# Last modulation row in buffers of its own, input splits at step 1, and the second new chunk packed in the new periods, in a spectral GEGLU block

## The chip, the cores and the metric

The program runs on one core of a Trainium2 chip. The metric is the device time of one execution in microseconds (us), the median of several runs of the same kernel.

## The reference, cut to what matters

```python
# x: (1, 1, 8192, 448); c: (1, 448)
mod = (silu(c) @ w_mod).reshape(1, 6, 1, 448)
sa, ca, ga, sb, cb, gb = mod[:, 0], ..., mod[:, 5]
h = layernorm(x) * (1 + ca) + sa
x = x + ga * spectral(h)          # rfft over 8192 positions, a 2-layer block MLP per frequency, irfft
h = layernorm(x) * (1 + cb) + sb
x = x + gb * ((gelu(h @ w_gate) * (h @ w_up)) @ w_down)     # 448 -> 1792 -> 448
```

`gb` is the last of the six modulation rows. It scales the output of the second half, the GEGLU network.

## The kernel before, in words

The program has four stretches. **The forward transform and the frequency MLP** go through 32 units (a half of the channels and a group of frequencies each). They are software-pipelined by `step(i)`, and `at(i, hook, fn, ...)` hangs other work on a step: loads, the scaling and splitting of the GEGLU weights into a high and a low float16 part (tiles `wk`), sums of the down weights. Steps 17 to 31 use the pool `fp` for the raw weights. `drain()` ends the pipeline.

**The turn** to the second half is straight code at the end of the listing. It finishes the inverse transform for chunk 0 in two halves of the channels: `inverse` (a matmul of the frequency data `v` with `g`), `residual`, `stats2`, `rsqrt0`, then the normalised rows `norm2` (tile `n`), `pack_hi` and `pack_lo` (the float16 high and low parts of `n` in tile `pk`), and `transposes` on TensorE into `nt`. In between stands `load_mod_row` for row 5: two DMAs into tiles `raw` of the pool `fp`, issued after the second half of the inverse, and right behind it `mod_half("gb", ...)`, eight matmuls on them. `down_hi` and `down_lo` split the down weights of one block `t` into `wd`, each in two instructions (672 and 896 elements a row).

**Eight plain chunks** (i = 0 to 7, 256 tokens each) follow. Each has 14 steps `gate_up(i, k)` of 20 matmuls (`pgu`), with a gelu on ScalarE, a product on VectorE (`x`, in `gate_up_out`), sums on GpSimd (`sums`) and `quantize` (ScalarE, then VectorE, into `ac`) for each pair of steps. After step 2 stands `down(i - 1)`: the down product of the chunk before (`pdn`), whose partial results leave through `p`, `u`, `o`. The work that prepares a coming chunk is hung on steps by the tables `hooks` (chunks 1 to 5) and `soon` (6 and 7): an entry `3: [(2, split_g), (2, split_v)]` means that after step 3 of chunk i the splits of chunk i + 2 are put into the queues. `split_g` and `split_v` cut `g` and `v` into a high part (ScalarE, `gh`, `vh`) and a low part (GpSimd, `gl`, and `v` in place); `inverse` at step 6 multiplies them in three matmuls a half (lines 1018 to 1020), the last of which takes the low part of `v`. `load_v` and `load_g` fetch the data for it.

**Twenty-four new chunks** (i = 8 to 31) use another scheme of seven periods each. `period(u)` puts its instructions into the queues in a fixed order: on TensorE 32 matmuls (`stage_a`), then later stages of the periods before, and `stage_b`, which can only follow once ScalarE has copied the bank out (`copy_b`, tile `sb`, line 1378). These chunks take more operands a row: `token_sums` makes differences of the two token halves (`tf`, VectorE and one GpSimd copy), `wpack_hi` (ScalarE) and `wpack_lo` (GpSimd) fill `pk`, and `wtransposes` issues five DMA transposes from `pk` into `nt`. The table `extra` hangs this work on the periods. Chunk 8 is the first new chunk and chunk 9 the second; before the change, both are packed at steps 12 and 13 of the plain chunks 6 and 7 (table `soon`, with `pack_rest`).

Every engine takes its instructions in the order in which the code emits them, so the tables set that order; SyncE's queue takes all DMAs. One `pk` tile serves all chunks.

Of the kernel before, what the change touches and what calls it, by code (L numbers as in the profile page):

```python
# [10 lines left out]
F32 = mybir.dt.float32  # L11
F32R = mybir.dt.float32r
F16 = mybir.dt.float16
# [6 lines left out]
D = 448  # L20
# [3 lines left out]
HC = 224  # L24
CB = 2
# [24 lines left out]
def spectral_geglu(ctx, tc, x, w1, b1, w2, b2, wg, wu, wd, cvec, wmod, cf1, cs2, cmi, cgm, out):  # L50
# [276 lines left out]
    with ExitStack() as bctx:  # L327
# [225 lines left out]
        def at(i, hook, fn, *args):  # L553
            side.setdefault((i, hook), []).append((fn, args))
# [112 lines left out]
        def load_mod_row(pool, q):  # L667
            out = []
            for hh in range(2):
                if pool is None:  # L670
                    wm = bp1.tile([128, GB, HC], F32, tag="tr", name="tr", bufs=2)[:112]
                elif callable(pool):
# [4 lines left out]
                dma(wm, wmod[:, c0 : c0 + HC].rearrange("(k p) c -> p k c", p=112))  # L677
                out.append(wm)
            return out
# [215 lines left out]
        }  # L895
        t0 = ep.tile([128, CB], F32, name="t0")

        def load_d(t, a, b):
# [46 lines left out]

        def down_lo(t):
            for r, k in zip(draws.pop(t), (slice(0, 3), slice(3, 7))):
                V.scalar_tensor_tensor(
                    wds[t][:, 1, k], r, dsc[:, t : t + 1], wds[t][:, 0, k], op0=ALU.mult, op1=ALU.subtract
                )  # L950
# [24 lines left out]
    with ExitStack() as cctx:  # L975
# [3 lines left out]
        x1s += [cp.tile([128, CB, D], F32, name=f"x1{n}") for n in (1, 2)]  # L979
        pkt = cp.tile([128, NXT * 128], F16, name="pk")  # L980
        nts, acts, pgu, outs = {}, {}, {}, []

# [60 lines left out]
        def rsqrt0(i):  # L1043

            mvt = nxt[i]["mv"]
            r, t = nxt[i]["r"][0], t0
            S.activation(r, mvt[:, :, 1], AF.Sqrt, bias=eps)
# [236 lines left out]
        def token_sums(i, part):  # L1284

            n = nxt[i]["n"]
            if part == 0:
                nxt[i]["t"] = cq.tile([128, 2 * D], F32, tag="o", name="tf") if i < NSTD + 2 else cp2.tile([128, 2 * D], F32, tag="tf", name="tf")
            t = nxt[i]["t"]
            b11, b21, x0 = n[:, 0, 0:192], n[:, 0, 192:384], n[:, 0, 384:448]  # L1290
            b12, b22, x1 = n[:, 1, 0:192], n[:, 1, 192:384], n[:, 1, 384:448]
            t1, t2, t3, t4 = (t[:, o : o + 192] for o in (0, 192, 384, 640))
            if part == 0:
                V.tensor_tensor(t1, b12, b11, ALU.subtract)
                V.tensor_tensor(t3, b22, b12, ALU.subtract)
                G.tensor_copy(t[:, 576:640], x1)
            else:
                V.tensor_tensor(t2, b22, t1, ALU.subtract)
                V.tensor_tensor(t4, b21, t2, ALU.subtract)
                V.tensor_tensor(t[:, 832:896], x0, x1, ALU.subtract)  # L1300

        def pieces(i, k):

            n, p = nxt[i]["n"], pkt
            if k == 0:
# [23 lines left out]
        def wtransposes(i, gs, w=5):  # L1329
            if i not in nts:  # L1330
                nts[i] = nt_tile()
            for g in gs:
                nc.sync.dma_start(
                    nts[i][:, w * g : w * g + w, :], pkt[:, 128 * w * g : 128 * w * (g + 1)], transpose=True
                )
# [161 lines left out]

        def pack_rest(i):
            if i == NSTD:
                wpack_hi(i, [3, 4])  # L1500
                wpack_lo(i, [3, 4])
            else:
                held.extend([(f, i, [k]) for k in (3, 4) for f in (wpack_hi, wpack_lo)])

        def pack(i):
# [124 lines left out]
        for n, k in enumerate((4, 7, 11, 13)):  # L1630
# [4 lines left out]
            5: [(1, turn)],  # L1635
            3: [(2, split_g), (2, split_v)],
            6: [(2, inverse)],
# [17 lines left out]
        soon = {  # L1655
            3: [(2, split_g), (2, split_v)],
            5: [(1, turn)],
            6: [(2, inverse)],
            7: [(2, residual)],
            8: [(2, stats2), (2, rsqrt_part, 5)],  # L1660
            9: [(2, rsqrt_part, 9)],
            10: [(2, norm2, 0)],
            11: [(2, norm2, 1)],
            12: [(2, token_sums, 0), (2, wpack_hi, [0, 1]), (2, wpack_lo, [0, 1])],
            13: [(2, token_sums, 1), (2, wpack_hi, [2]), (2, wpack_lo, [2]), (2, pack_rest)],
        }

# [67 lines left out]
        for i in range(NSTD):  # L1735
# [4 lines left out]
            for k in range(NFT):  # L1740
# [14 lines left out]
                if k == 4:  # L1755
                    store_out()
                if (i, k) == (NSTD - 1, 9):
                    load_v(NSTD + 2)
                    load_g(NSTD + 2)
                for fn, *args in first.pop(i * NFT + k, []):  # L1760
                    fn(*args)
                if k == (3, 1, 0)[min(i, 2)] and i + 2 < nch:
                    load_v(i + 2)
                    load_g(i + 2)
                for d, fn, *args in (hooks if i < NSTD - 2 else soon).get(k, []):
                    if i + d > 2 and i > 0 and i + d < nch:
                        fn(i + d, *args)
# [7 lines left out]
        sets = [sets[(n - U0) % 3] for n in range(3)]  # L1775
        pdn = [psum2.tile([128, 512], F32, name=f"pdn{n}") for n in range(2)]
        x1s.append(cp2.tile([128, CB, D], F32, name="x13"))

        for u in range(U0, NT_ + 1):
            period(u)  # L1780
# [5 lines left out]
            flush()  # L1786
            for d, fn, *args in extra[k]:
                if i + d < nch:
# [88 lines left out]
```

## Time and profile before

| | us |
|---|---|
| median of 3 runs | 1911.73 (1910.2 to 1912.13) |
| the profiled execution's own time | 1911.48 |
| its span | 1909.7 |
| TensorE busy in the span | 1858.1 |
| VectorE, GpSimd, ScalarE busy | 1433.6, 1264.3, 995.4 |
| the turn: first to last matmul of the inverse for chunk 0 to the first `pgu` | from 368.20 to 384.88 |
| the plain chunks' last `pgu` to the first matmul of the new scheme | from 770.00 to 773.83 |

Times in the trace are us from the start of the span. A row of the timeline gives the start, the time from start to end, the engine, the source line, what it writes and reads, how many instructions are merged in it, and in brackets the idle time of the engine before it with what ended that. Rows of the waits give the waiting line, what it waited for, the total, the number of waits and the longest. A row of the windows gives a stretch, its length, the busy time of the engines and, behind them, the TensorE clock that was granted (1.00 is full speed), the share of the DMA engines and GB/s.

### The profile page before, as it was taken

To read this page: it belongs to the slowest core of one execution; us is meant where nothing else is said; L and a number is where in the kernel's file an instruction comes from. 1 tells how busy PE (TensorE), PEld (TensorE's weight loads), DVE (VectorE), ACT (ScalarE), POOL (GpSimd) and SP (SyncE) were. 2 spreads that over 40 slices of the span, in tenths; PEclk is the share of its full clock that TensorE was granted. 3 is DMA by queue.
4 is the path that set the end of the run, shared out by engine and by line. 5 is a ranking of instruction groups with operands and counts; after the bars stand their busy time and mean duration, and the time that the engine had idled before them with its cause. 6 is when DMAs were issued, how large, how long until landed. Compare 5 with 4: busy or idle time off the path is not lost.

```text
span 1909.7 us, 56500 instructions
## 1 busy us (share of the span) xinstructions
PE 1858.1 (97%) x23332; PEld 1756.6 (92%) x23332; DVE 1433.6 (75%) x2888; ACT 995.4 (52%) x1843; POOL 1264.3 (66%) x1616
## 2 busy tenths in 40 slices
PE   7899999899999999899999999999999999999998
PEld 3599999778888888899999999999999999999998
DVE  8677788778766667577777777777777777777645
ACT  5687888653444444345545555555555454444443
POOL 3157655247777777577777777777777777777533
PEclk9999999999999999899999999999999999999999
DMA  9998777645434445866666665556666666666641
GB/s 353 319 291 260 203 181 196 172 135 141 104 101 102 101 90 132 230 178 175 171 180 176 177 167 166 166 166 166 167 175 179 168 176 178 169 182 178 156 140 54
DMA packets 380602, 330.49 MB, mean 173 GB/s; under 512 B 110772, under 2 KB 358712, under 8 KB 380344
## 3 DMA queue, kind: packets, MB, share of 16 engines
q1 hardware_dynamic: 380344, 326.87, 61.6%
q8 instruction: 183, 3.00, 0.6%
q14 instruction: 75, 0.61, 0.1%
HBM read 243.32 MB, written 60.10 MB: 159 GB/s over the span
## 4 chain that ended last, share of the span: by engine, by line
PE 78%; DVE 7%; POOL 5%; DMA 4%; issue 3%; ACT 2%; SPq 1%; ACTq 0%; POOLq 0%; DVEq 0%
PE set L1350 38%; PE pgu L1118 8%; PE pdn L1193 6%; PE pdn L1191 6%; PE pdn L1192 6%; PE set L1191 2%; PE set L1193 2%; PE set L1192 2%; PE ps L210 2%; DMA xt<-in_A_x 2%; DVE y L471 1%; POOL v L115 1%; DMA s<-cs 1%; POOL yl L115 1%; PE set L1460 1%
## 5 line engine op out<-in xcount | busy, mean ns | idle before, releaser
L1350 PE MATMUL set<-nt,wk 128*128 128x128 f16 x13104 | 745.4, 220 | 8.8 <-DVE x L1159 3.8
L1350 PEld LDWEIGHTS <-wk 128*128 128x128 f16 x13104 | 738.6, 98 | 13.7 <-issue 11.6
L1193 PE MATMUL pdn<-wd,ac 128*128 128x224 f16 x1218 | 316.4, 260 | 1.8 <-DVE ac L1425 1.2
L1191 PE MATMUL pdn<-wd,ac 128*128 128x224 f16 x1218 | 316.6, 260 | 0.7 <-ACT ac L1415 0.6
L1192 PE MATMUL pdn<-wd,ac 128*128 128x224 f16 x1218 | 316.4, 260 | 0.0
L1118 PE MATMUL pgu<-nt,wk 128*128 128x256 f16 (+1 forms) x2464 | 268.2, 274 | 2.7 <-DVE x L1159 2.6
L1118 PEld LDWEIGHTS <-wk 128*128 128x128 f16 (+1 forms) x2464 | 225.7, 98 | 43.7 <-issue 17.9
L1399 ACT ACTIVATE gl<-c,dg 128x384 f32<-128x384 f32 x168 | 103.6, 616 | 253.5 <-DVE c L1393 252.4
L1425 DVE SCALAR_TENSOR_TENSOR ac<-x,sa_act,ac 128x896 f16<-128x896 f32 x168 | 211.5, 1259 | 14.7 <-ACT ac L1415 14.7
L1167 POOL TENSOR_TENSOR x<-x 128x128 f32<-128x128 f32 x223 | 136.3, 611 | 118.2 <-DVE x L1159 50.7
L1234 POOL TENSOR_TENSOR o<-u,p 128x224 f32<-128x224 f32 x32 | 21.0, 658 | 260.6 <-DVE u L1233 260.6
L1403 DVE TENSOR_TENSOR x<-c,gl 128x384 f32<-128x384 f32 x168 | 175.9, 1047 | 17.1 <-ACT gl L1399 17.1
L1415 ACT ACTIVATE ac<-x,sa_act 128x896 f16<-128x896 f32 x168 | 173.7, 1034 | 3.4 <-DVE x L1170 0.4
L1170 POOL TENSOR_TENSOR x<-x 128x128 f32<-128x128 f32 x223 | 170.6, 765 | 0.1
L1191 PEld LDWEIGHTS <-ac 128*128 128x128 f16 x1568 | 153.6, 98 | 5.9 <-issue 4.8
L1193 PEld LDWEIGHTS <-ac 128*128 128x128 f16 x1568 | 153.6, 98 | 2.8 <-DVE ac L1425 1.7
L1192 PEld LDWEIGHTS <-ac 128*128 128x128 f16 x1568 | 153.6, 98 | 0.6 <-issue 0.3
L1169 POOL TENSOR_TENSOR x<-x 128x128 f32<-128x128 f32 x223 | 148.3, 665 | 0.0
L1387 DVE TENSOR_TENSOR c<-set,sb 128x512 f32<-128x512 f32 x168 | 114.9, 684 | 43.1 <-PE set L1350 43.1
L1154 ACT ACTIVATE gel<-pgu,dg 128x256 f32<-128x256 f32 x112 | 49.9, 471 | 158.3 <-PE pgu L1118 148.3
L471 DVE SCALAR_TENSOR_TENSOR y<-pm,t 64x224 f32<-64x224 f32 x256 | 99.4, 388 | 39.1 <-ACT t L463 35.1
L1168 POOL TENSOR_TENSOR x<-x 128x128 f32<-128x128 f32 x223 | 113.8, 510 | 17.5
(323 smaller groups left out, 3992.2 us busy)
## 6 DMA issues: line engine op xcount, KB each, us to landing
wk<-wk SPq DMA_DIRECT2D x76, 1024.0 KB, 9.4
wk<-wk SPq DMA_DIRECT2D x76, 768.0 KB, 5.7
tr<-td SPq DMA_DIRECT2D x64, 224.0 KB, 4.5
vd<-us SPq DMA_DIRECT2D x64, 224.0 KB, 3.2
xx<-in_A_x SPq DMA_DIRECT2D x32, 448.0 KB, 5.9
v<-vd SPq DMA_DIRECT2D x63, 224.0 KB, 5.2
out<-x SPq DMA_DIRECT2D x31, 448.0 KB, 3.6
xt<-in_A_x SPq DMA_DIRECT2D x15, 896.0 KB, 16.5
```

The source lines that it names most:

```text
L471: V.scalar_tensor_tensor(y[ri * 64 : ri * 64 + 64, gi], pv[si, ri], LAM, tv[si, ri], op0=ALU.add, op1=ALU.min)
L1118: T.matmul(pgu[i, t, q][:, pr * H : (pr + 1) * H], ws[rows, n, w, tw], nts[i][rows, tn, :], start=start, stop=stop, skip_group_check=True,)
L1167: e.tensor_tensor(s1, a21, a22, ALU.add)
L1169: e.tensor_tensor(s3, a11, a21, ALU.subtract)
L1170: e.tensor_tensor(s4, a12, s2, ALU.subtract)
L1191: T.matmul(ps, ac[:, 0, ka], w[:, 0, kb], start=n == 0, stop=False)
L1192: T.matmul(ps, ac[:, 0, ka], w[:, 1, kb], start=False, stop=False)
L1193: T.matmul(ps, ac[:, 1, ka], w[:, 0, kb], start=False, stop=n == NP - 1)
L1350: T.matmul(ps2[:, pr, reg * 128 : reg * 128 + 128], slot[:, pr, hl, wt, :], nt[:, xt, :], start=start and j == 0, stop=j == len(terms) - 1 ...
L1403: V.tensor_tensor(xs[u][:, 1::3, :], cts.pop(u)[:, 1], gls.pop(u), ALU.mult)
L1415: S.activation(ac[:, 0], xs[u][:, 0:7], AF.Copy, scale=sa_act[:, t : t + 1])
L1425: V.scalar_tensor_tensor(ac[:, 1], xs.pop(u)[:, 0:7], sa_act[:, t : t + 1], ac[:, 0], op0=ALU.mult, op1=ALU.subtract)
```

## The change

- Row 5 of the modulation weights gets two tiles of its own (`gbw`, in the pool `fp`) and its two DMAs stand in step 29.
- `rsqrt0` runs a Gelu on two elements a row right behind its Sqrt (into `g0`, which nothing reads).
- In the turn, `norm2`, `pack_hi` and `pack_lo` of chunk 0 stand ahead of the loads for what follows, and the second instruction of `down_lo(0)` stands behind `pack_lo`.
- In the plain chunks the splits stand at step 1 in place of step 3, and the loads for them at step 9 of the chunk before (chunk 3 keeps its places).
- `token_sums` and packing of chunk 8 stand at steps 0 and 1 of chunk 7; statistics and normalisation of chunks 8 and 9 stand one step later each.
- Chunk 9 is packed in periods 0 and 1 of chunk 8 (table `opening`), into a second tile `pk2`; from then on the two `pk` tiles take turns. Its five transposes stand together in period 2.

```diff
+        gbw = [fp.tile([112, 4, HC], F32, name=f"gbw{h}") for h in range(2)]
+        at(29, "load", pre, gbw, "gb", load_mod_row, 5)
...
             S.activation(r, mvt[:, :, 1], AF.Sqrt, bias=eps)
+            S.activation(g0, mvt[:, :, 1], AF.Gelu_apprx_tanh)
...
-        down_lo(0)
+        down_lo(0, range(1))
         inverse(0, halves[1])
-        pre(fp, "gb", load_mod_row, 5)
         for hh in range(2):
             mod_half("gb", gb, hh)
         residual(0, halves[1])
         stats2(0, halves[1])
         rsqrt0(0)
+        for b in range(CB):
+            norm2(0, b)
+        pack_hi(0)
+        pack_lo(0)
+        down_lo(0, range(1, 2))
         fctx.close()
...
         for t in (1, 2):
             load_d8(t)
-        for b in range(CB):
-            norm2(0, b)
-        pack_hi(0)
         S.copy(gb_r, gb[:, :D])
-        pack_lo(0)
...
         hooks = {
-            3: [(2, split_g), (2, split_v)],
+            1: [(2, split_g), (2, split_v)],
...
         soon = {
-            3: [(2, split_g), (2, split_v)],
+            0: [(1, token_sums, 0), (1, token_sums, 1), (1, wpack_hi, range(3)), (1, wpack_lo, range(3))],
+            1: [(1, wpack_hi, [3, 4]), (1, wpack_lo, [3, 4]), (2, split_g), (2, split_v)],
...
-            10: [(2, norm2, 0)],
-            11: [(2, norm2, 1)],
-            12: [(2, token_sums, 0), (2, wpack_hi, [0, 1]), (2, wpack_lo, [0, 1])],
-            13: [(2, token_sums, 1), (2, wpack_hi, [2]), (2, wpack_lo, [2]), (2, pack_rest)],
+            11: [(2, norm2, 0)],
+            12: [(2, norm2, 1)],
...
-                if k == (3, 1, 0)[min(i, 2)] and i + 2 < nch:
+                if (i, k) in ((0, 3), (1, 1)):
                     load_v(i + 2)
                     load_g(i + 2)
+                if i == 1 and k == 3:
+                    split_g(3)
+                    split_v(3)
+                if k == 9 and i > 0:
+                    load_v(i + 3)
+                    load_g(i + 3)
...
+        pkts.append(cp2.tile([128, NXT * 128], F16, name="pk2"))
...
+        opening = {
+            0: [(2, split_v), (1, token_sums, 0), (1, token_sums, 1), (1, wpack_hi, [0, 1]), ...],
+            1: [(2, split_g), (1, wpack_hi, [3]), (1, wpack_lo, [3]), (1, wpack_hi, [4]), (1, wpack_lo, [4])],
+            2: [(1, wtransposes, range(5))],
+        }
...
-            for d, fn, *args in extra[k]:
+            for d, fn, *args in opening[k] if i == NSTD and k < 3 else extra[k]:
```

How the order of the instructions moves is seen at three places. The first is ScalarE's queue in the turn, from the copy of the row `ga` to the first gelu of the plain chunks (`r` is the Sqrt of `rsqrt0`, `pk` the packing, `nt` the copy of a transpose, `wd` from `dr` the down weights of blocks 1 and 2). Before:

```order
L1692 COPY ga_r<-psm 128x224
L1047 ACTIVATE r_3372<-mv_3371,eps 128x2
L1073 CAST pk<-n_5824 128x448 x2
L1712 COPY gb_r<-psm 128x448
L1111 CAST nt<-ptr 128x512 x2
L944 ACTIVATE wd_5740<-dr,dsc 128x672
L944 ACTIVATE wd_5740<-dr,dsc 128x896
L944 ACTIVATE wd_5741<-dr,dsc 128x672
L944 ACTIVATE wd_5741<-dr,dsc 128x896
L1154 ACT_TABLE_LOAD
L1154 ACTIVATE gel<-pgu,dg 128x256 x4
```

And after:

```order
L1695 COPY ga_r<-psm 128x224
L1053 ACTIVATE r_3372<-mv_3371,eps 128x2
L1054 ACT_TABLE_LOAD
L1054 ACTIVATE g_3374<-mv_3371 128x2
L1080 CAST pk<-n_5801 128x448 x2
L1716 COPY gb_r<-psm 128x448
L1118 CAST nt<-ptr 128x512 x2
L947 ACTIVATE wd_5745<-dr,dsc 128x672
L947 ACTIVATE wd_5745<-dr,dsc 128x896
L947 ACTIVATE wd_5746<-dr,dsc 128x672
L947 ACTIVATE wd_5746<-dr,dsc 128x896
L1161 ACTIVATE gel<-pgu,dg 128x256 x4
```

The load of the activation table has moved from ahead of the first gelu to ahead of the packing.

The second is GpSimd's queue around `down(5)` in the plain chunk 6: `wr` and `wf` are sums for the new scheme's weights, `o` and the `x` of 448 elements the end of the down product, the `x` of 128 elements the sums of a pair of steps. Before:

```order
L1532 TENSOR_TENSOR wr<-wr,wf 128x384
L1533 TENSOR_TENSOR wf<-wr,wf 128x384
L1234 TENSOR_TENSOR o<-u_10013,p_10012 128x224
L1205 TENSOR_TENSOR o<-o,gb_r 128x448
L1206 TENSOR_TENSOR x_5747<-o,x_5747 128x448
L1205 TENSOR_TENSOR o<-o,gb_r 128x448
L1206 TENSOR_TENSOR x_5747<-o,x_5747 128x448
L1167 TENSOR_TENSOR x_10007<-x_10007 128x128
L1168 TENSOR_TENSOR x_10007<-x_10007 128x128
L1169 TENSOR_TENSOR x_10007<-x_10007 128x128
L1170 TENSOR_TENSOR x_10007<-x_10007 128x128
L115 TENSOR_TENSOR gl<-g,gh 128x256
```

And after:

```order
L115 TENSOR_TENSOR gl<-g,gh 128x256
L115 TENSOR_TENSOR v<-v,vh 128x896
L1535 TENSOR_TENSOR wr<-wr,wf 128x384
L1536 TENSOR_TENSOR wf<-wr,wf 128x384
L1241 TENSOR_TENSOR o<-u_10022,p_10021 128x224
L1212 TENSOR_TENSOR o<-o,gb_r 128x448
L1213 TENSOR_TENSOR x_5752<-o,x_5752 128x448
L1212 TENSOR_TENSOR o<-o,gb_r 128x448
L1213 TENSOR_TENSOR x_5752<-o,x_5752 128x448
L1174 TENSOR_TENSOR x_10016<-x_10016 128x128
```

The two low parts, `gl` and `v`, have moved from behind eleven instructions to ahead of them.

The third is ScalarE's queue where the new scheme opens (`ac` is the quantizing of the last pair of plain steps, `sb` the copies of three periods, `set` the seed copies, `vh` and `gh` the split for chunk 10). Before:

```order
L1178 ACTIVATE ac<-x_11246,sa_act 128x896
L1321 CAST pk<-n_11213 128x256
L1178 ACTIVATE ac<-x_11284,sa_act 128x896
L1321 CAST pk<-tf 128x2x192
L1321 CAST pk<-tf 128x2x256
L1378 COPY sb<-set_11343 128x512
L113 CAST vh<-v 128x896
L1382 COPY set_11343<-set_11343 128x2x128
L1378 COPY sb<-set_11344 128x512
```

And after:

```order
L1185 ACTIVATE ac<-x_11245,sa_act 128x896
L1185 ACTIVATE ac<-x_11284,sa_act 128x896
L1388 COPY sb<-set_11331 128x512
L113 CAST vh<-v 128x896
L1392 COPY set_11331<-set_11331 128x2x128
L1331 CAST pk_11336<-n_11259 128x192
L1331 CAST pk_11336<-n_11259 128x256 x2
L1388 COPY sb<-set_11332 128x512
L113 CAST gh<-g 128x256
L1392 COPY set_11332<-set_11332 128x2x128
L1331 CAST pk_11336<-tf 128x2x192
L1331 CAST pk_11336<-tf 128x2x256
```

The casts of the packing have moved from ahead of the first `sb` to behind it. GpSimd's queue has moved in the same way: its four packing instructions that stood ahead of the last pair's sums, and the others, now stand behind them.

More of the change, by code (lines that the diff above doesn't have):

```diff
@@ L896, in spectral_geglu @@
         t0 = ep.tile([128, CB], F32, name="t0")
+        g0 = ep.tile([128, CB], F32, name="g0")
         def load_d(t, a, b):
@@ L944, in down_hi, with down_lo @@
                 S.activation(wds[t][:, 0, k], r, AF.Copy, scale=dsc[:, t : t + 1])
-        def down_lo(t):
-            for r, k in zip(draws.pop(t), (slice(0, 3), slice(3, 7))):
+        def down_lo(t, ns=range(2)):
+            for r, k in list(zip(draws[t], (slice(0, 3), slice(3, 7))))[ns.start : ns.stop]:
                 V.scalar_tensor_tensor(
@@ L980, in spectral_geglu @@
         pkt = cp.tile([128, NXT * 128], F16, name="pk")
+        pkts = [pkt]
         nts, acts, pgu, outs = {}, {}, {}, []
@@ L1287, in token_sums @@
             if part == 0:
-                nxt[i]["t"] = cq.tile([128, 2 * D], F32, tag="o", name="tf") if i < NSTD + 2 else cp2.tile([128, 2 * D], F32, tag="tf", name="tf")
+                nxt[i]["t"] = cq.tile([128, 2 * D], F32, tag="o", name="tf") if i < NSTD + 1 else cp2.tile([128, 2 * D], F32, tag="tf", name="tf")
             t = nxt[i]["t"]
@@ L1300, in token_sums, with pk_of @@
                 V.tensor_tensor(t[:, 832:896], x0, x1, ALU.subtract)
+        def pk_of(i):
+            return pkts[max(0, i - NSTD) % 2]
         def pieces(i, k):
-            n, p = nxt[i]["n"], pkt
+            n, p = nxt[i]["n"], pk_of(i)
             if k == 0:
@@ L1333, in wtransposes @@
                 nc.sync.dma_start(
-                    nts[i][:, w * g : w * g + w, :], pkt[:, 128 * w * g : 128 * w * (g + 1)], transpose=True
+                    nts[i][:, w * g : w * g + w, :], pk_of(i)[:, 128 * w * g : 128 * w * (g + 1)], transpose=True
                 )
@@ L1496, in spectral_geglu @@
         }
[L1498 to L1503, printed above, removed]
         def pack(i):
@@ L1776, in spectral_geglu @@
         pdn = [psum2.tile([128, 512], F32, name=f"pdn{n}") for n in range(2)]
+        pkts.append(cp2.tile([128, NXT * 128], F16, name="pk2"))
         x1s.append(cp2.tile([128, CB, D], F32, name="x13"))
+        opening = {
+            0: [
+                (2, split_v),
+                (1, token_sums, 0),
+                (1, token_sums, 1),
+                (1, wpack_hi, [0, 1]),
+                (1, wpack_lo, [0, 1]),
+                (1, wpack_hi, [2]),
+                (1, wpack_lo, [2]),
+            ],
+            1: [(2, split_g), (1, wpack_hi, [3]), (1, wpack_lo, [3]), (1, wpack_hi, [4]), (1, wpack_lo, [4])],
+            2: [(1, wtransposes, range(5))],
+        }
         for u in range(U0, NT_ + 1):
```

14 lines of the change are left out of this document (8 added, 6 removed).

## The prediction, made before the changed kernel ran

> **What bounds the kernel now.** I read the waits of TensorE first, then the timeline around each of the three edits, engine by engine.
>
> ```profile
> PE psm L683 <- DMA raw<-in_w_mod: 6.0, 1, 6.0
> PE set L1350 <- DVE x L1159: 3.8, 1, 3.8
> PE pi L1020 <- POOL v L115: 3.6, 7, 0.6
> PE set L1350 <- ACT sb L1378: 3.6, 1, 3.6
> PE pgu L1118 <- DVE x L1159: 2.6, 1, 2.6
> ```
>
> By the table above TensorE is busy for 1858.1 us of the span of 1909.7, so only its pauses can be won, and a slow clock behind them. The rows give five such waits: one in the turn (6.0), one behind it that the turn's work feeds (2.6), seven short ones in the plain chunks (3.6 together) and two at the opening of the new scheme (3.8 and 3.6). Together they are 19.6 us; each edit stands beside one of them. The question is how much of each remains because something else is nearly as late.
>
> **The turn.** TensorE's and SyncE's rows:
>
> ```profile
> 377.85 5.49 PE L683 MATMUL psm<-raw,cs 112*128 112x224 f32 x16 [5.99 <-DMA raw<-in_w_mod]
> ...
> 384.88 7.76 PE L1118 MATMUL pgu<-nt,wk 128*128 128x256 f16 x68
> ...
> 408.55 16.66 PE L1118 MATMUL pgu<-nt,wk 128*128 128x256 f16 x140 [2.58 <-DVE x L1159]
> ```
>
> ```profile
> 372.60 1.34 SPq L677 DMA_DIRECT2D raw<-in_w_mod  x2
> ...
> 383.41 0.37 SPq L899 DMA_DIRECT2D dr<-in_B_w_down  x1
> ```
>
> The row gb was issued at 372.60 and its matmuls began at 377.85. With the load at step 29 they follow the inverse at once, and the 5.99 us are gone as a wait. They are not gone from the end: the transposes of `pk` come next on TensorE, and they wait for VectorE.
>
> ```profile
> 380.31 0.55 DVE L1082 TENSOR_TENSOR pk<-n,pk 128x384 f16<-128x384 f32 x1
> ...
> 389.99 1.15 DVE L948 SCALAR_TENSOR_TENSOR wd<-dr,dsc,wd 128x896 f16<-128x896 f32 x1 [1.87 <-ACT wd L944]
> ...
> 393.75 0.79 DVE L1159 TENSOR_TENSOR x<-pgu,gel 128x256 f32<-128x256 f32 x2 [0.36 <-ACT gel L1154]
> ```
>
> The last low part of `pk` was done at 380.31 + 0.55 = 380.86. The part of `down_lo(0)` that leaves the front of this queue has the 896 elements a row of 389.99, 1.15 us there (1.1 below), so `pk` is complete at about 379.8. Then the moved instruction runs, to 380.9, and VectorE's cast of the transposed rows into `nt` is queued behind it. Before, the first `pgu` came 1.54 us after the end of the matmuls for gb (377.85 + 5.49 = 383.34, then 384.88); that gives 379.8 + 1.5 = 381.3, and 0.7 more for the cast that waits behind the moved instruction: 382.0, 2.9 us earlier.
>
> What that is worth at the end is decided by the 2.58 us at 408.55, where TensorE waits for VectorE again. So the term goes by VectorE's chain, which begins with the down weights `dr`.
>
> ```profile
> 375.21 0.29 ACT L1047 ACTIVATE r<-mv,eps 128x2 f32<-128x2 f32 x1 [4.19 <-DVE mv L1041]
> ...
> 378.29 0.57 ACT L1073 CAST pk<-n 128x448 f16<-128x448 f32 x1 [2.79 <-DMA raw<-in_w_mod]
> ...
> 388.91 1.79 ACT L944 ACTIVATE wd<-dr,dsc 128x896 f16<-128x896 f32 x2 [1.75 <-DMA dr<-sd]
> ...
> 391.95 1.28 ACT L1154 ACT_TABLE_LOAD   x1
> ...
> 393.25 0.84 ACT L1154 ACTIVATE gel<-pgu,dg 128x256 f32<-128x256 f32 x2
> ```
>
> ScalarE waits for `dr` (1.75 at 388.91) and VectorE for ScalarE (1.87 at 389.99). The first of these loads was issued at 383.41, behind the gb row. Now it waits for the moved low part, at about 381.0: 2.4 us earlier, and the chain with it. The table load no longer lies between the last `wd` and the first gelu; VectorE was only kept idle by it for 0.36 us (393.75), since its own `wd` work ended then. That adds 0.4. At its new place the table load is covered: the Sqrt ends 1.1 us earlier, at 374.4; 1.28 and a Gelu of 0.29 (the Sqrt's row has the same size) end at 376.0, ahead of the first cast to `pk`, due at 378.29 - 1.1 = 377.2. If that cover were gone, the whole Gelu and load would cost 1.6.
>
> The Trainium skill ("ScalarE: Activation LUTs", section "What ACT_TABLE_LOAD costs") counts some 1.3 us for a load and about as much for the drain ahead of it. The trace shows the 1.28, and the gelu 0.02 behind it; a drain would show as idle time and there is none here. By the page ScalarE would be ready at about 377.4, 0.2 late, and the term would be 2.6.
>
> The 0.8 MB of early gb load falls in units 29 and on; what it could delay there I take as nothing, as the raw weights of that stretch are issued some microseconds ahead of their use, and a delay of the last would show in the turn's first matmuls. Sum of the turn: **2.8 us**. Lower bound 0.7: the slow clock after the pause.
>
> ```profile
> 377.85:382.80 4.95, 4.95 (x15) 0.55 0.76 228
> 409.00:413.00 4.00, 4.00 (x24) 0.58 1.04 222
> 774.00:785.00 11.00, 7.42 (x79) 0.54 0.88 279
> ```
>
> These windows give the length, TensorE's busy time, the granted clock, DMA share and GB/s. After a pause TensorE runs at 0.55 for 4.95 us, 2.2 us of loss. Now the pause lies between gb and the transposes, so part of this loss falls on the first `pgu`: 2.9 - 2.2 = 0.7. Upper bound 4.5: if the stall of 408.55 gets too short to slow the clock, the 0.42 x 4.0 = 1.7 us of the second row go as well.
>
> **The plain chunks.** One inverse of chunk 6, and GpSimd's rows:
>
> ```profile
> 701.70 0.45 PE L1018 MATMUL pi<-vh,gh 128*128 128x448 f32 x1
> 701.99 0.37 PE L1019 MATMUL pi<-vh,gl 128*128 128x448 f32 x1
> 702.88 0.47 PE L1020 MATMUL pi<-v,gh 128*128 128x448 f32 x1 [0.53 <-POOL v L115]
> ```
>
> ```profile
> 689.63 1.10 POOL L1533 TENSOR_TENSOR wf<-wr,wf 128x384 f32<-128x384 f32 x1 [3.69 <-DVE ws L1568]
> ...
> 700.05 0.73 POOL L115 TENSOR_TENSOR gl<-g,gh 128x256 fp32r<-128x256 f32 x1
> 700.73 2.09 POOL L115 TENSOR_TENSOR v<-v,vh 128x896 fp32r<-128x896 f32 x1
> ```
>
> The third product starts 0.89 us after the second, which started 0.29 after the first; without the wait the spacing would be 0.29, so 0.60 a chunk. The low part ended at 700.73 + 2.09 = 702.82, and the third product came 0.06 later. Six of the seven waits go, since chunk 3 keeps its places: 6 x 0.60 = **3.6 us**; by the idle time alone 6 x 3.6/7 = 3.1; if the seventh went too, 4.2. Cover: the two low parts (0.73 + 2.09 = 2.8 us) now stand ahead of `wr`, `wf` and the down product's `o` on GpSimd, where it idled 3.69 us ahead of 689.63. If that gap were filled, the sums of the next pair would be 2.8 later. The loads: a step is 20 matmuls, at 7.76/68 = 0.114 each 2.3 us, and from step 9 to step 1 are six steps, 13.7 us; the gb row above, issued at 372.60, was in use 5.25 us later. On SyncE they stand ahead of later loads and wait for the buffer that step 6 of the same chunk releases, three steps earlier.
>
> **The opening.** TensorE, VectorE, GpSimd and ScalarE:
>
> ```profile
> 773.83 2.67 PE L1350 MATMUL set<-nt,wk 128*128 128x128 f16 x32 [3.83 <-DVE x L1159]
> ...
> 780.07 11.14 PE L1350 MATMUL set<-nt,wk 128*128 128x128 f16 x154 [3.58 <-ACT sb L1378]
> ...
> 806.43 23.76 PE L1350 MATMUL set<-nt,wk 128*128 128x128 f16 x419
> ```
>
> ```profile
> 772.57 0.34 DVE L1294 TENSOR_TENSOR tf<-n 128x192 f32<-128x192 f32 x1
> 773.37 0.41 DVE L1159 TENSOR_TENSOR x<-pgu,gel 128x256 f32<-128x256 f32 x1
> ```
>
> ```profile
> 772.59 0.64 POOL L1170 TENSOR_TENSOR x<-x 128x128 f32<-128x128 f32 x1
> ...
> 774.78 1.30 POOL L1167 TENSOR_TENSOR x<-x 128x128 f32<-128x128 f32 x1
> ```
>
> ```profile
> 777.58 1.04 ACT L1178 ACTIVATE ac<-x,sa_act 128x896 f16<-128x896 f32 x1 [2.98 <-POOL x L1170]
> 778.53 1.01 ACT L1321 CAST pk<-tf 128x384 f16<-128x384 f32 x2
> 779.45 0.57 ACT L1378 COPY sb<-set 128x512 f32<-128x512 f32 x1
> ```
>
> ```profile
> 769.00:782.00 13.00, 0.00 (x0) 0.00 (x0) 0.00 (x0) 2.04 (x5) 4.72 (x7) 0.73 0.98 312
> ```
>
> The last product of the plain chunks began at 773.37, behind the differences `tf` of chunk 9, which began at 772.57. Without them it starts 0.80 earlier and ends at 773.0; the first seed matmul goes with it. The sums began at 774.78, behind packing on GpSimd. Now they can begin when the sums of the pair before end, 772.59 + 0.64 = 773.2: 1.6 earlier, and so ScalarE's `ac`, which waited 2.98 us for them. Then come two casts less ahead of `sb`, 779.45 - 778.53 = 0.9. So `sb`, and TensorE at 780.07, come 1.6 + 0.9 = **2.5 us** earlier, at about 777.6. The seed matmuls that `sb` copies end at 773.0 + 2.7 = 775.7, in time. Next late is GpSimd's sums. Lower bound 0.9, the casts alone, if sums go no faster. Upper bound 4.2, with half of what the slow clock takes at 774 to 785 (7.42 x 0.46 = 3.4) won; only half, since the first wait there shrinks from 3.83 to about 3.0 and remains.
>
> The packing comes back in the next two periods: the last window row (tile `pk`: TensorE's two, VectorE's, ScalarE's and GpSimd's busy time) has 2.04 us of ScalarE and 4.72 of GpSimd. TensorE's stretch of 154 matmuls is 11.14 us long; both fit beside it. If they did not, all 2.04 would return through `sb` and only 0.5 would remain.
>
> **The sum.** 2.8 + 3.6 + 2.5 = 8.9. The profiled execution took 1911.48 us, of which 1909.7 is the span; 1911.48 - 8.9 = **1902.6 us**. It lies 0.25 below the median of the runs shown, whose spread is 1.9, so I correct nothing.
>
> **The rivals.**
>
> *The clock no longer drops* (chance 0.25). The stalls get shorter: at 408.55 to 2.58 + 2.9 - 2.8 = 2.7 at most, and to 0.5 if the slow clock takes its 2.2 us earlier, from the first `pgu`. For it: with waits of 0.53 us the plain chunks show no such loss. Against: 2.58 was enough to give the 0.58 of 409 to 413. It would bring 1.7 there and 1.7 at the opening: 1902.6 - 3.4 = 1899.2 us. The Trainium skill ("TensorE: Matmul & The Clock Gate", section "What's actually happening") has the array idle for about a whole 3.4 us window before the clock is lowered. By that rule a stall of 2.58 us would do nothing; the measured 0.58 behind it speaks against reading it so strictly.
>
> *The moved splits cost what they win* (0.10). The 2.8 us on GpSimd delay the end of the down product or the sums, and TensorE waits 0.6 a chunk elsewhere. Against: the 3.69 us idle. All of 3.6 is lost: 1906.2 us.
>
> *The turn gains nothing* (0.10). The edit does not do what it says: the inputs of the `dr` loads come from elsewhere than the issue at 383.41, and VectorE's chain arrives as before; an earlier first `pgu` then only lengthens the stall. For it: that stall exists. 1902.6 + 2.8 = 1905.4 us.
>
> *Chunk 9's transposes come too late* (0.05; the other side).
>
> ```profile
> 792.08 7.92 SPq L1333 DMA_TRANSPOSE nt<-pk  x4
> ...
> 809.08 0.53 SPq L1269 DMA_DIRECT2D wk<-wk  x1
> ```
>
> They now stand together in period 2. If a weight load that waits for its buffer (as that at 809.08) stood ahead of them on SyncE, the third, at 7.92/4 = 1.98 each, would start at 809.1 + 4.0 + 2.0 = 815.0. The seed matmuls of chunk 9 follow 806.43 and need it 2.7 earlier, at 803.7, by the 2.7 us that 32 of them take: 11.3 us of wait and, as after the turn, 2.2 of clock, 1902.6 + 13.5 = 1916.1 us. It decides from a third transpose issued some 9 us late, 812.6. Against: the order of the code has the load that waits behind the five; they wait for GpSimd's packing alone, done by about 788.
>
> **How the numbers follow.** My forecast has 0.50, the rivals 0.25, 0.10, 0.10 and 0.05. A measurement of this kernel can tell 0.2%, 3.8 us, from no change: 1907.9 and 1915.5. The forecast by its bounds: lower ends of turn and opening together give 1902.6 + 2.1 + 1.6 = 1906.3, upper ends of all three 1911.5 - 4.5 - 4.2 - 4.2 = 1898.6. The range 1897.5 to 1907.5 holds this, the clock's rival with 1.7 more, and the two at 1905 to 1906 alone; outside are the last rival and combinations of the two lost terms. Faster by over 0.2% are all but these: 0.90; within 0.2% are the combinations, 0.05; slower 0.05.
>
> **What would show it.** In the turn: gb's matmuls without a wait, then a pause until about 379.8 and the first `pgu` near 382; `dr` issued near 381; the wait on VectorE near 405.8. In the plain chunks: one wait of L1020's kind in place of seven, and no new wait at the down product. At the opening: `sb` right behind `ac`, and TensorE resuming 2.5 us sooner than the shift so far gives. It is wrong if `dr` isn't earlier, if GpSimd's sums start as late as before, or if a new wait stands at the seeds of chunk 9.

## The result, and the profile after

The changed kernel takes 1904.06 us (median of 5 runs, 1902.93 to 1905.44) beside 1911.73 of the kernel before; the ratio is 0.9961, with a 95% interval of 0.9946 to 0.9975. Run again later it gave 0.9966 (0.9953 to 0.9978). The forecast was 1902.6, 8.9 us less than before; measured are 7.7 less. The profiled execution is the fastest of the five, 1902.93 us with a span of 1901.1. Of the runs below, one of the eleven with the turn alone took 4517.27 us, far from all others, and is left out of its ratio.

TensorE's waits after:

```profile
PE ptr L1107 <- ACT pk L1080: 4.5, 2, 3.5
PE pdn L1198 <- DVE u L1234: 3.6, 2, 2.1
PE set L1360 <- DVE x L1166: 3.3, 1, 3.3
PE pgu L1125 <- DVE x L1166: 1.8, 1, 1.8
...
PE set L1360 <- ACT sb L1388: 0.7, 1, 0.7
PE pi L1026 <- POOL v L115: 0.6, 1, 0.6
```

The wait for gb is gone (a wait for `pk` stands in its place), the seven for `v` are one, and `sb` is down from 3.6 to 0.7 (2.3 in the second trace of this kernel, see below). A new one stands second: 3.6 us in two waits of the down product for `u`.

To see where time went, I cut both traces at the same instructions. Before:

```profile
368.96 1.68 PE L683 MATMUL psm<-tr,cs 112*128 112x224 f32 x8
456.37 0.45 PE L1018 MATMUL pi<-vh,gh 128*128 128x448 f32 x1
752.63 0.36 PE L1018 MATMUL pi<-vh,gh 128*128 128x448 f32 x1
791.02 0.45 PE L1460 MATMUL set<-vh,gh 128*128 128x448 f32 x1
1864.72 0.66 POOL L1234 TENSOR_TENSOR o<-u,p 128x224 f32<-128x224 f32 x1 [13.37 <-DVE u L1233]
1903.57 0.67 POOL L1234 TENSOR_TENSOR o<-u,p 128x224 f32<-128x224 f32 x1 [6.74 <-DVE u L1233]
```

And after:

```profile
369.04 1.68 PE L685 MATMUL psm<-tr,cs 112*128 112x224 f32 x8
453.59 0.45 PE L1024 MATMUL pi<-vh,gh 128*128 128x448 f32 x1
748.31 0.36 PE L1024 MATMUL pi<-vh,gh 128*128 128x448 f32 x1
784.09 0.45 PE L1470 MATMUL set<-vh,gh 128*128 128x448 f32 x1
1858.12 0.66 POOL L1241 TENSOR_TENSOR o<-u,p 128x224 f32<-128x224 f32 x1 [13.36 <-DVE u L1240]
1895.33 0.67 POOL L1241 TENSOR_TENSOR o<-u,p 128x224 f32<-128x224 f32 x1 [5.22 <-DVE u L1240]
```

The cuts are the last matmuls for ga, the inverse of chunk 3, that of chunk 9 (second half), that of chunk 10, and the last two `o` of the program. Five stretches lie between them. Here they are for every trace of this study; a difference of starts in each case:

| | start to ga | turn | plain chunks | opening | new chunks | tail |
|---|---|---|---|---|---|---|
| before | 368.96 | 87.41 | 296.26 | 38.39 | 1073.70 | 38.85 |
| before, again | 371.33 | 88.20 | 296.34 | 37.31 | 1073.87 | 37.21 |
| changed | 369.04 | 84.55 | 294.72 | 35.78 | 1074.03 | 37.21 |
| changed, again | 370.02 | 85.35 | 293.02 | 35.13 | 1074.02 | 38.82 |
| turn alone | 369.39 | 84.40 | 296.36 | 38.32 | 1073.99 | 38.78 |
| splits alone | 368.94 | 87.41 | 291.58 | 37.43 | 1074.06 | 37.21 |
| opening alone | 370.14 | 87.31 | 296.10 | 35.73 | 1074.15 | 37.21 |
| `tf` first | 371.75 | 84.08 | 292.15 | 35.13 | 1074.00 | 38.78 |
| own gb buffers alone | 372.20 | 83.62 | 296.23 | 37.65 | 1073.80 | 38.85 |
| `down_lo` whole | 371.71 | 83.59 | 293.00 | 35.27 | 1073.78 | 37.21 |
| no Gelu ahead | 370.26 | 85.62 | 294.71 | 35.72 | 1073.98 | 37.21 |
| first combination | 370.48 | 81.63 | 297.10 | 35.15 | 1074.00 | 38.78 |
| `down_lo` and `tf` | 371.70 | 84.14 | 292.16 | 35.14 | 1073.99 | 38.85 |
| second combination | 371.51 | 82.20 | 295.83 | 33.51 | 1073.99 | 38.83 |

Between the first traces of before and after the turn gives 2.9, the plain chunks 1.5, the opening 2.6, and the tail 1.6, where the change does nothing. The start and the tail differ between two executions of one kernel by as much (368.96 and 371.33; 38.85 and 37.21): that is chance, and the other columns carry the comparison. They are not free of it either: the turn of two traces of one kernel differs by 0.8 us, the opening by up to 1.1.

### The profile page after: what moved, and what is told of

Its sections match the earlier page's. It is cut to its first block, busy times and chain, and to the rows that moved or that the text cites. A ratio compares the mean times of both kernels' runs of the same rounds, so it can differ in the third digit from the quotient of the medians.

```text
span 1901.1 us, 56363 instructions
## 1 busy us (share of the span) xinstructions
PE 1855.4 (98%) x23332; PEld 1756.8 (92%) x23332; DVE 1428.5 (75%) x2888; ACT 996.1 (52%) x1844; POOL 1266.1 (67%) x1616
## 4 chain that ended last, share of the span: by engine, by line
PE 78%; DVE 11%; DMA 4%; ACT 2%; POOL 2%; SPq 2%; issue 1%; ACTq 0%; DVEq 0%; POOLq 0%
PE set L1360 34%; PE pgu L1125 11%; PE pdn L1198 6%; PE pdn L1200 6%; PE pdn L1199 6%; PE set L1198 2%; PE set L1200 2%; PE set L1199 2%; PE ps L210 2%; DMA xt<-in_A_x 2%; DVE y L471 1%; DVE x L1413 1%; DMA raw<-in_B_w_up 1%; DVE c L1397 1%; DVE wk L826 1%
```

## The experiments

**One part at a time.** Three kernels have one part of the change each; a fourth is the changed kernel with one exchange in the table `soon`:

```diff
-            0: [..., (1, wpack_hi, range(3)), (1, wpack_lo, range(3))],
-            1: [(1, wpack_hi, [3, 4]), (1, wpack_lo, [3, 4]), (2, split_g), (2, split_v)],
+            0: [..., (1, wpack_hi, [3, 4]), (1, wpack_lo, [3, 4])],
+            1: [(1, wpack_hi, range(3)), (1, wpack_lo, range(3)), (2, split_g), (2, split_v)],
```

*The turn alone.*

> The kernel before with the turn's edits alone (own gb buffers, Gelu behind the Sqrt, packing ahead of the loads, down_lo divided). Theory: VectorE's chain from the dr loads sets the gain, so TensorE resumes at about 406.1 where it waited until 408.55, 2.4 us earlier; a further 1.7 us appear where the clock stays full behind that stall, but 1.3 of it are given back as a wait for u at the first down product. Net 2.8 us, about 1908.9. Rival: the turn's whole advance, 4.1 us, stays to the end, about 1907.6.

Measured: 1908.87 us, 0.9980 (0.9971 to 0.9989). The medians can't choose between 2.8 and 4.1 us: the ratio's interval is 2.1 to 5.5 us. The trace speaks for the theory: its turn is 3.0 us shorter than before's, and the wait at the first down product is there (1.4).

*The splits alone.*

> The kernel before with the splits at step 1 and their loads at step 9 alone. Theory: 0.78 us for each of six inverses, 4.7 us, about 1907.0, and no new wait at the down products. Rival 1 (the forecast): 0.60 each, 3.6 us, 1908.1. Rival 2: GpSimd's 2.8 us ahead of the down product's end cause the new wait of 2.1 us for u in chunk 7, so that the gain is only 1.6 us, 1910.1.

Measured: 1904.42 us, 0.9960 (0.9948 to 0.9973), more than any theory. In the stretch of the plain chunks it is 296.26 - 291.58 = 4.7 us, as the theory has it, with no wait for `u` in chunk 7. The rest of its trace's lead is 1.0 us at the opening and 1.6 in the tail, both places where the clock differs. What else the runs have in their favour stays open.

*The opening alone.*

> The kernel before with the packing edits alone (chunk 8 at steps 0 and 1 of chunk 7, chunk 9 in the new periods, second pk tile). Theory: the first output of the down product in chunk 7 has to wait for the buffer in which the differences tf of chunk 8 lie until GpSimd has packed them; that costs 3.1 us, the opening itself gains 2.5, so it is slower by 0.6 us, about 1912.3. Rival (the forecast): only the 2.5 us gain, 1909.2, and no wait for u in chunk 7.

Measured: 1908.38 us, 0.9976 (0.9967 to 0.9985). Faster, so the theory's sum was wrong.

```profile
736.98 0.39 DVE L1220 TENSOR_TENSOR o<-pdn,p 128x224 f32<-128x224 f32 x1 [5.50 <-POOL pk L1331]
```

```profile
738.94 0.26 PE L1192 MATMUL pdn<-wd,ac 128*128 128x224 f16 x1 [0.57 <-DVE u L1228]
```

VectorE does wait for `tf`'s packing ahead of the `o` of `down(6)`, 5.50 us, but TensorE waits for `u` only 0.57, about as long as before waits there for `ac` (0.62 in all). The plain chunks take 296.10 us, no more than before's 296.26: the buffer costs only where the splits have moved too. Why is seen behind `o`: two instructions `ws` take 1.29 us here, and GpSimd runs `wr` beside them.

```profile
737.29 1.29 DVE L1572 SCALAR_TENSOR_TENSOR ws<-wr,sww,ws 128x128 f16<-128x128 f32 x2
```

```profile
736.90 1.01 POOL L1536 TENSOR_TENSOR wr<-wr,wf 128x384 f32<-128x384 f32 x1
```

*`tf` first.*

> The changed kernel with chunk 8's two packing groups exchanged: the pieces from tf at step 0, those from the normalised rows at step 1. The same work on GpSimd and ScalarE, but the buffer of tf is free some 4 us earlier. Theory (the buffer): VectorE's wait of 5.5 us ahead of the first output of down(6) shrinks to about 1 us, the 2.1 us wait for u goes with the slow clock behind it, 3.1 us less than the changed kernel, about 1901. Rival (GpSimd is simply too full there): nothing changes, about 1904.

Measured: 1902.49 us, 0.9948 (0.9936 to 0.9961). The two kernels' rows for the buffer, the changed kernel first:

```profile
726.92 2.17 POOL L1337 TENSOR_TENSOR pk<-tf,pk 128x128 f16<-128x128 f32 x3
729.73 2.12 POOL L115 TENSOR_TENSOR v<-v,vh 128x896 fp32r<-128x896 f32 x1
```

```profile
729.12 0.39 DVE L1226 TENSOR_TENSOR o<-pdn,p 128x224 f32<-128x224 f32 x1 [5.49 <-POOL pk L1337]
729.43 2.84 DVE L1571 SCALAR_TENSOR_TENSOR ws<-wr,sww,ws 128x128 f16<-128x128 f32 x2
732.19 0.38 DVE L1234 TENSOR_TENSOR u<-pdn,p 128x224 f32<-128x224 f32 x1
```

```profile
732.62 0.26 PE L1198 MATMUL pdn<-wd,ac 128*128 128x224 f16 x1 [2.12 <-DVE u L1234]
```

```profile
728.00:735.00 7.00, 4.88 (x46) 0.90 0.01 3
735.00:738.00 3.00, 3.00 (x23) 0.66 0.94 197
```

With `tf` first:

```profile
723.92 2.18 POOL L1337 TENSOR_TENSOR pk<-tf,pk 128x128 f16<-128x128 f32 x3
```

```profile
729.05 0.39 DVE L1226 TENSOR_TENSOR o<-pdn,p 128x224 f32<-128x224 f32 x1
```

```profile
727.52 0.27 PE L1200 MATMUL pdn<-wd,ac 128*128 128x224 f16 x1 [1.17 <-DVE ac L1186]
```

The tile `tf` of chunk 8 and the output `o` of a down product share one buffer (`tag="o"`). In the changed kernel GpSimd ends the packing from `tf` at 729.09, VectorE's `o` follows at 729.12 after 5.49 us without work, then `ws` (2.84), and `u` comes at 732.19, for which TensorE stands still for 2.12 us; the two windows (length, TensorE's busy time, clock) show the slow clock behind. The two `ws` take 1.55 us longer (2.84) than in the kernel with the opening alone, and by as much (2.12 against 0.57) TensorE's wait is longer. The second of them takes 2.42 us in the four traces in which the moved split `v` runs on GpSimd beside it (the changed kernel twice, `down_lo` whole, no Gelu ahead), and 0.60 to 0.81 in the ten others; it ends 0.4 us after `v` (732.27 and 731.85). So the wait needs both edits; that `v` slows `ws` is read from this agreement alone, as no run moves `v` by itself. In the other order the packing ends at 726.1 and `o` has almost no wait (0.13), at the same work; `v` then runs behind both `ws`, and TensorE waits 1.17 us for `ac` in place of 2.12 for `u`. The plain chunks take 292.15 us, against 294.72 and 293.02 in the changed kernel: the order costs 0.9 to 2.6 us, the larger where the clock drops behind the wait.

**The clock.** The kernel before, unchanged:

> The kernel before once more, unchanged. In its first trace the last 39 us took 38.85 us from the last-but-one to the last o, with the clock at 0.8 behind two waits of 0.6 and 1.0 us; the changed kernel's trace has 37.21 with the same waits at full clock. Theory (the clock behind such waits is chance of the execution): the tail comes out at 37.2 or 38.8, and the clock behind the wait of 2.58 us at 408.5 full or slow, independently of the kernel. Rival (it belongs to the kernel): 38.85 and the slow clock at 409 to 413 again.

Measured: 1912.15 us (one run). The rival falls: the tail took 37.21 us and the clock behind the wait was full.

```profile
411.87 1.36 PE L1118 MATMUL pgu<-nt,wk 128*128 128x256 f16 x11 [2.58 <-DVE x L1159]
```

```profile
411.90:416.00 4.10, 4.10 (x38) 1.00 0.95 240
```

The wait for VectorE was 2.58 us again, as in the trace that had 0.58 behind it; the window (length, TensorE's busy time, clock) has 1.00. In the tail the two waits (0.6 and 1.0) are in all traces; the windows of TensorE behind them in the first trace of before, and in the changed kernel:

```profile
1892.00:1900.00 8.00, 6.88 (x53) 0.79 0.04 14
```

```profile
1885.00:1893.00 8.00, 6.82 (x68) 1.00 0.04 14
```

Eight of the fourteen traces have the long tail, six the short one. The wait for `u` of 2.1 us in chunk 7 shows the same: in the first trace of the changed kernel and without the Gelu ahead the clock behind it is 0.6 and the plain chunks take 294.7 us, in the second trace and with `down_lo` whole it is 1.00 and they take 293.0.

**The turn's parts.** The kernel before with the own gb buffers and nothing else:

```diff
+        gbw = [fp.tile([112, 4, HC], F32, name=f"gbw{h}") for h in range(2)]
+        at(29, "load", pre, gbw, "gb", load_mod_row, 5)
...
-        pre(fp, "gb", load_mod_row, 5)
```

> The kernel before with the own buffers of the gb row alone, nothing else moved. Theory: the loads dr are freed by gb's matmuls, so they start at about 376.3 in place of 383.4, ScalarE's and VectorE's wd work follows the nt casts without a wait, the stall at 408.5 goes and TensorE's earlier start by some 2.4 us stays: 4 to 5 us at 408.5, more than the whole turn's 2.4, because nothing is queued ahead of dr. Rival (the forecast's order of causes): the packing sets the first pgu and the dr loads gain nothing by it alone, at most 1 us.

And the changed kernel with `down_lo(0)` whole, at its old place:

> The changed kernel with down_lo(0) whole at its old place. Theory: the dr loads wait in the changed kernel for the moved instruction alone (381.44, issue at 381.53); whole, they start at about 376.3, the stall of 1.77 us at 406.1 goes, and TensorE gains 1.5 to 2 us there although pk is up to 0.6 us later. Rival: pk 1.1 us later delays the first pgu by as much, and the loads are no earlier: 1 us slower.

Measured: 1908.09 us, 0.9977 (0.9968 to 0.9986), and 1902.24, 0.9942 (0.9929 to 0.9954). SyncE's first `dr` in the changed kernel, with the VectorE instruction that frees it, then in the two others:

```profile
381.53 0.37 SPq L902 DMA_DIRECT2D dr<-in_B_w_down  x1
```

```profile
380.30 1.14 DVE L951 SCALAR_TENSOR_TENSOR wd<-raw,dsc,wd 128x896 f16<-128x896 f32 x1
```

```profile
379.06 0.42 SPq L901 DMA_DIRECT2D dr<-in_B_w_down  x1
```

```profile
378.56 0.42 SPq L902 DMA_DIRECT2D dr<-in_B_w_down  x1
```

Counted from the ga matmuls, `dr` starts after 12.5 us in the changed kernel, 14.4 before, 6.9 in both others. So the moved half of `down_lo(0)` holds the `dr` loads back. The turn is 83.6 us in both, 0.9 to 1.8 less than in the changed kernel, but this gain is hardly clear of chance: over all traces, those with `down_lo(0)` whole and own buffers have 81.6 to 84.1 (83.6 to 84.1 where nothing else in the turn is moved), those with all the turn's edits 84.1 to 85.4, and the ratio of the own buffers alone (0.9977) can't be told from that of the whole turn (0.9980). The stall that was to go is still there, 1.07 us in both. Neither gives the 4 to 5 us, or the 1.5 to 2, in full, since TensorE then waits at the first down product for `u` (1.72 and 1.40 us), which VectorE's normalisation of chunk 2 sets: the first combination below moves it, and has no such wait.

The changed kernel without the Gelu ahead:

> The changed kernel without the Gelu behind the Sqrt, so that the table load stands ahead of the first gelu again. Theory: ScalarE's first gelu comes 1.28 us later, VectorE's first product only 0.4 us later, since its own wd work ends then: 0.4 us at the wait near 406. Rival: the load lies on the path, 1.3 us there or, with a drain of the engine, 2.6.

```profile
391.68 1.28 ACT L1160 ACT_TABLE_LOAD   x1
392.97 0.84 ACT L1160 ACTIVATE gel<-pgu,dg 128x256 f32<-128x256 f32 x2
```

```profile
393.48 0.79 DVE L1165 TENSOR_TENSOR x<-pgu,gel 128x256 f32<-128x256 f32 x2 [0.44 <-ACT gel L1160]
```

One run, 1905.12 us. VectorE waits 0.44 us ahead of its first product, where the changed kernel has no wait. TensorE's wait ends 0.9 us later from the ga matmuls (408.26 - 370.26 against 406.14 - 369.04), of which 0.3 are already in the last `dr` cast on ScalarE: about 0.5 for the table load, as the theory has it. Counted from that cast the wait ends 17.6 us later, and 16.9 to 17.1 later in the four traces with the Gelu ahead and the same order otherwise. That these 0.5 us last to the end of the program, one run can't show.

**Combinations.** The changed kernel again, for comparison, and three steps beyond it:

> The changed kernel once more, unchanged, beside the combination. Theory: its own figures again, 0.996 of the kernel before; between the turn's last ga matmuls and the inverse of chunk 3 84.6 us, from there to the inverse of chunk 9 294.7 with the slow clock behind the wait for u or 293.0 without it, the last two o 37.2 or 38.8 apart.

Measured: 1905.44 us, 0.9966. Its plain chunks took 293.0 us, without the slow clock, and its turn 85.35, 0.8 more than in the first trace. The first combination has `down_lo(0)` whole, `tf` first, and this:

```diff
-            "down": [(norm2, 0), (norm2, 1)],
-            "down2": [(pack_hi,), (pack_lo,), (transposes_dma, range(1))],
+            "down": [],
+            "down2": [(norm2, 0), (norm2, 1), (pack_hi,), (pack_lo,), (transposes_dma, range(1))],
```

> The changed kernel with down_lo(0) whole at its old place, chunk 8's pieces from tf packed first, and, in chunk 1, the normalisation of chunk 2 behind the down product's middle in place of ahead of it. Theory: the first two give 1.0 us in the turn and 1.4 to 2.6 in chunk 7, and the third takes away the wait of 1.4 us for u at the first down product: 4 to 5 us below the changed kernel, about 0.9935 of the kernel before. Rival: the third is worth nothing, since the normalisation then delays the transposes of chunk 2 or TensorE waits for VectorE in the next step: 2.4 to 3.6 us.

Measured: 1904.53 us, 0.9959 (0.9946 to 0.9973): no better. The wait for `u` is gone and the turn 2.9 us shorter than in the first changed trace, but the plain chunks take 297.10:

```profile
454.79 0.47 PE L1025 MATMUL pi<-vh,gl 128*128 128x448 f32 x1 [2.23 <-POOL gl L115]
456.83 0.47 PE L1026 MATMUL pi<-v,gh 128*128 128x448 f32 x1 [1.57 <-POOL v L115]
```

The later packing of chunk 2 delays GpSimd's split for chunk 3, and its inverse waits 3.8 us. The next kernel leaves the third edit out.

> The changed kernel with down_lo(0) whole at its old place and chunk 8's pieces from tf packed first, and nothing else. Theory: 83.6 us from the last ga matmuls to the inverse of chunk 3 (84.6 to 85.4 in the changed kernel), 292.1 to the inverse of chunk 9 (293.0 to 294.7), 35.1 behind: some 2 to 3.5 us below the changed kernel, 0.994 to 0.995 of the kernel before. Rival: the two don't add up, and it is no faster than the changed kernel.

Measured: 1900.93 us, 0.9940 (0.9928 to 0.9953), as the theory has it; only the turn took 84.14 in place of 83.6. The last one moves the normalisation again, and the packing with it:

```diff
-            "down": [(norm2, 0), (norm2, 1)],
-            "down2": [(pack_hi,), (pack_lo,), (transposes_dma, range(1))],
+            "down": [],
+            "down2": [(norm2, 0), (norm2, 1)],
+            4: [(pack_hi,), (pack_lo,), (transposes_dma, range(2))],
...
-                    if i == 1:
-                        transposes_dma(2, range(1, 2))
```

> As the run before it, with the normalisation of chunk 2 behind the down product's middle, and its packing and transposes at step 4, behind the split for chunk 3. Theory (in the first combination GpSimd's packing of chunk 2 stood ahead of the split for chunk 3 and cost 3.8 us at the inverse): the waits of 2.2 and 1.6 us at that inverse go, and 81.6 us in the turn stay: 1.5 to 2 us less again than dlo_tf, 0.993 to 0.994. Rival: the low parts are late for another reason, and the inverse of chunk 3 waits over 2 us as before.

Measured: 1900.01 us, 0.9938 (0.9924 to 0.9952). `gl`'s wait is gone, but `v`'s is 1.69 and a new wait for VectorE of 1.81 us stands in chunk 2: no clear gain on the run before it. Both medians lie 3 to 5 us below the changed kernel's two; their intervals overlap that of its first measurement a little (0.9946 to 0.9953) and at most touch that of its second (from 0.9953). They have the lowest medians here, but can't be told apart, nor from `down_lo` whole (0.9942) and `tf` first (0.9948).

## Why the prediction was right, point by point

The time lies in the range, and the gain of 7.7 is near the 8.9 of the forecast. The three places and what releases TensorE there were right, but that the total came so near is partly luck: the splits were worth 1.1 us more than forecast, and a wait that the forecast left out took 1.4 to 3.1. The terms came out like this:

- **The turn, 2.8 forecast, 2.9 in the trace.** The first `pgu` came at 382.44 (382.0 said), `dr` at 381.53 (381.0), TensorE resumed at 406.14 (405.8). The chain was the one given: `dr`, held by the moved half of `down_lo(0)`. Counted from the ga matmuls TensorE resumed 2.5 us earlier there; the 2.9 came about by two further amounts that nearly cancel (the rival with the clock, below), so the agreement to 0.1 is luck. What I did not draw from the chain is that this half holds the `dr` loads back by 5.6 us, so that the own buffers alone gain as much.
- **The plain chunks, 3.6 forecast, 4.7 by the splits alone.** The step that failed is the spacing of 0.29 that the third product was to fall back to. One inverse of chunk 6 after:

```profile
695.81 0.45 PE L1024 MATMUL pi<-vh,gh 128*128 128x448 f32 x1
696.11 0.36 PE L1025 MATMUL pi<-vh,gl 128*128 128x448 f32 x1
696.31 0.36 PE L1026 MATMUL pi<-v,gh 128*128 128x448 f32 x1
696.51 0.37 PE L1024 MATMUL pi<-vh,gh 128*128 128x448 f32 x1
```

  From the first product to the second half it is 0.70 us, before 1.48 (from 701.70 to 703.18, where the second half starts there): 0.78 a chunk, not 0.60. Only the first of a row of these products takes 0.29; the others follow at 0.20, and after the wait the next one paid that again.
- **The opening, 2.5 forecast, 2.6 in the trace** (1.5 to 2.2 against the second trace of before, which had less slow clock there). `sb` stands right behind `ac`:

```profile
771.70 1.04 ACT L1185 ACTIVATE ac<-x,sa_act 128x896 f16<-128x896 f32 x1 [3.23 <-POOL x L1177]
772.65 0.58 ACT L1388 COPY sb<-set 128x512 f32<-128x512 f32 x1
```

```profile
773.28 11.01 PE L1360 MATMUL set<-nt,wk 128*128 128x128 f16 x154 [0.72 <-ACT sb L1388]
```

  Behind it TensorE resumed 24.97 us after the cut in chunk 9 (773.28 - 748.31), before 27.44 (780.07 - 752.63): 2.5 earlier, as forecast, and 2.5 in the second traces too (24.94 and 27.45). The length of the wait says less: 0.7 us in the first trace and 2.3 in the second, since the 32 matmuls ahead of it took 3.57 and 1.95 us.
- **The missing term.** I gave no price to moving chunk 8's packing behind the start of chunk 7, and wrote that no new wait would stand at the down product. The shared buffer of `tf` and `o` makes one, 2.12 us together with the `ws` that runs beside the moved split. In the first trace the plain chunks gained 296.26 - 294.72 = 1.5 in place of the 4.7 of the splits alone, so this term took 3.1 us, the slow clock behind the wait included; in the second trace it took 1.4. The second rival named the place and, it seems, half of the cause: the moved split is one of the two things that the wait needs, but with the splits alone, or the packing alone, there is none of this length.
- **The rival with the clock.** The clock behind the turn's wait stayed full, and TensorE was 4.1 us ahead at the inverse of chunk 2, not 2.4:

```profile
426.79 1.67 PE L1013 MATMUL pi<-v,g 128*128 128x448 f32 x4
```

```profile
422.72 1.29 PE L1019 MATMUL pi<-v,g 128*128 128x448 f32 x3
```

```profile
440.26 0.26 PE L1198 MATMUL pdn<-wd,ac 128*128 128x224 f16 x1 [1.44 <-DVE u L1234]
```

  But it isn't the shorter stall that does it: an unchanged kernel kept its clock behind 2.58 us. And it was worth little: 1.3 of the 1.7 us were given back at the first down product, where the changed kernel waited 1.44 for `u`, and the one before 0.15 (behind its slow clock):

```profile
443.04 0.26 PE L1191 MATMUL pdn<-wd,ac 128*128 128x224 f16 x1 [0.15 <-DVE u L1227]
```

  Other traces with the turn of before bear this out. With the slow clock (before, the splits alone) the turn takes 87.41 us in both; with the full clock (before again, the opening alone) TensorE waits 1.65 and 1.80 us for `u`, and the turn takes 88.20 and 87.31. So this slow clock was worth next to nothing in the end.

  The Trainium skill ("TensorE: Matmul & The Clock Gate", section "What's actually happening") says that the window in which activity is judged runs freely and doesn't start with the kernel; that the same wait ends both ways here agrees with it. The same section has the clock go down after at least one idle window of about 3.4 us; that does not agree, for 0.79 stood here behind waits of 0.6 and 1.0 us.
- **The late transposes** did not come: after the inverse of chunk 10 no new wait stands in the trace, and the new chunks take 1074.0 us against 1073.7 and 1073.9.

What stays open is why the three parts measured alone sum to 0.2 + 0.4 + 0.2% = 0.8%, some 16 us, and the whole to 7.7. The stretches of their traces sum to 3.0 + 4.7 + 2.7 = 10.4 us, and the wait at the shared buffer takes 1.4 to 3.1 of that when splits and packing meet; the rest would have to be chance of start, clock and tail in the medians, which one trace each can't show.

## What to carry to other kernels

Before moving an instruction, look at which buffer it keeps and who is next to write it: a tile that shares its buffer with another by a tag makes a wait that no data dependency shows, and it is priced by when its last reader ends and by what the waiting engine still has to do behind it. When a wait goes, its whole row of instructions has to be compared with an undisturbed one, not just its idle time. And a gain is only kept up to the next place where another engine was nearly late: here one that waited 0.15 us took back 1.3.

## What the runs showed of the hardware

The granted clock behind the same wait of 2.58 us was 0.58 over 4 us in one execution of the same kernel and 1.00 in another; the 1.7 us that this made by the next inverse were gone at the next wait. Behind the wait of 2.1 us in chunk 7 it was 0.6 in two traces and 1.00 in two others, worth 1.7; behind waits of 0.6 and 1.0 us it was 0.79 in one and 1.00 in another, worth 1.6. A VectorE instruction `ws` of 0.60 to 0.81 us took 2.42 in the four traces in which GpSimd's `v` of 2.12 us ran beside it, and in no other. The time up to the turn differs between executions by up to 3.3 us (368.94 to 372.20), with no edit there but the early load of gb. A difference below 3 us in one trace of this kernel has to be read stretch by stretch.
